# LayerNorm and MLP on one core: tile 2 turned by VectorE, eight rows opened with tiles 0 and 1, tile 3 of twenty rows made up later

## The chip, the core and the metric

The kernel runs on one core of a Trainium2 chip. The metric is the device time of one execution in microseconds (us). In the names of the profile PE is TensorE, PEld its weight loads, DVE is VectorE, ACT is ScalarE, POOL is GpSimd and SP is SyncE, which issues most of the DMAs. All times of a trace count from the start of its span.

## The reference

```
def reference(x, w1, b1, w2, b2):      # x 2048 x 1024, w1 1024 x 3584, w2 3584 x 1024, bfloat16
    y = _layernorm(x, axis=-1)         # (x - mean) / sqrt(var + 1e-5)
    h = _gelu(jnp.einsum("bsd,df->bsf", y, w1) + b1)     # tanh approximation
    return jnp.einsum("bsf,fd->bsd", h, w2) + b2
```

## The kernel before

**Blocks, tiles, rows.** The 2048 positions of x are cut into 4 blocks of 512, a block into 4 tiles of 128. For each block the first product (helper `pe_cell`, L331) makes h transposed: 28 *rows* r of 128 features, each a PSUM bank of 128 x 512, the sum over 8 slices *dt* of the 1024 inputs. A matmul holds a 128 x 128 piece of w1 still and streams columns of the transposed input `yT_sb`; a column is a position, so a tile is 128 columns. ScalarE applies gelu and bias b1 (`act_gelu`, L351) and writes `hT_sb`. The second product (`out_chunk`, L380) sums over 28 rows into 128 x 512 pieces of the output, which VectorE adds b2 to (L391) and SP stores. The order on TensorE is: first product of block 0, second product of block 0, first of block 1, and so on.

**Queues.** The program is written as one list of operations for each engine, in order. An operation waits for named events of others; what stands behind it on its engine waits too. SP's list holds the loads: the halves of tiles 0 and 1 first, then 256 KB pieces of w1 (`w1_chunks`) with tiles 2 and 3 of x in between, b1, the rest of w1, block 1 of x, w2, b2 and the other blocks.

**The opening.** Block 0 is special, because its input has to be normalised and transposed while w1 still arrives. Tiles 0 to 3 are only centred before the product (`raw_tile`: a sum on VectorE at L413, a subtraction at L417, into `c_sb`); the division by the standard deviation comes after it. ScalarE's `square` (L423) or VectorE's statistics give the variance, GpSimd takes the power -0.5 (L236, L426, L429), and VectorE spreads the four tiles' results over all partitions into `rbc_sb` with transposes and copies (L462, L467, L472). When a row's bank is complete, VectorE multiplies it in place by `rbc_sb` (L348, event `rm_r`), and the gelu of the row waits for that. Ahead of rbc on VectorE stand the turn of b1 (L457) and its cast.

Tiles 0, 1 and 2 are transposed by TensorE (`pe_T`, L305; each group of slices is copied from PSUM by ScalarE, L311). Tile 3 is turned on VectorE by one instruction that transposes each 32 x 32 block (L439), and 16 copies of 32 partitions put the blocks in place, 8 on VectorE (L448), 8 on ScalarE (L453).

TensorE runs 39 matmuls on constants first (`fill`, L291). `OPEN` then lists the order: an entry (t, d0, d1) is tile t with slices d0 to d1 for the four rows of the first wave, an entry (t, None) the transposes of tile t. Rows 4 to 7 follow with tiles 0 to 2 together (384 columns), then tile 3 of rows 0 to 7, which completes them. Rows 8 to 27 take all 512 columns at once. A row takes a bank from `new_unit`: rows 0 to 7 the banks 0 to 7, later ones the six banks 0 to 5 in turn, waiting for the gelu that last read the bank.

**VectorE's planner.** From rm 0 on VectorE's order is planned on the host. `crit` holds the multiplications (later the b2 additions) with a due time, `fills` the normalisation and the turn of the next block with a release time; the planner takes the next of `crit` when its due time has come within 0.3 us of its own clock, otherwise the next of `fills`. Due times come from the estimate `est` of when TensorE completes the row.

Of the kernel before, what the change touches and what calls it, by code (L numbers as in the profile page):

```python
# [11 lines left out]
P = 128  # L12
# [4 lines left out]
R0 = 4  # L17
R1 = 8
N_FILL_A = 37
N_FILL_C = 2  # L20
OPEN = ((0, 0, 2), (1, None), (0, 2, 4), (0, 4, 6), (1, 0, 6), (0, 6, 8), (2, None), (1, 6, 8), (2, 0, 8))
CEN_0 = (0, 2, 8)
GROUPS_0 = ((0, 2, 7), (2, 5, 4), (5, 8, 5))
GROUPS_1 = ((0, 4, 6), (4, 8, 7))
GROUPS_2 = ((0, 2, 4), (2, 5, 5), (5, 8, 6))
COPY_ACT = ((0, 1), (0, 2), (0, 3), (1, 2), (1, 3), (2, 3), (3, 2), (2, 1))
NOB = 2
# [59 lines left out]
def bass_standalone__mixer_channel_mlp__prompt_kernel(  # L87
# [18 lines left out]
    HC = D // 2  # L106
    NRAW = TPB
    assert ST % TB == 0 and NB >= 2 and D % P == 0 and D & (D - 1) == 0 and F % P == 0 and D % NCH == 0
    assert HC <= 512 and DT == 8 and FT >= 8 and FT <= 32

    w1_chunks = [(j, j + 2, 0, 512) for j in range(0, DT, 2)] + [(j, j + 4, 512, 768) for j in (0, 4)]
    c0 = 768
    for wdt in (256, 512, 1024, 1024):
        if c0 + wdt <= F:
            w1_chunks.append((0, DT, c0, c0 + wdt))
            c0 += wdt
# [20 lines left out]
    with ExitStack() as es:  # L137
# [62 lines left out]
        for i in range(2):  # L200
            for h, q in enumerate((sp, act)):
                dma(x_sb[:, i, h * HC:(h + 1) * HC], xf[i * P:(i + 1) * P, h * HC:(h + 1) * HC],
                    f"x{i}_{h}", P * HC * 2, q)
        for ci in range(3):
            load_w1(ci)
        load_x_tile(2)
        load_w1(3)
        load_x_tile(3)
        load_w1(4)
        load_w1(5)  # L210
        sp.op(None, waits=["b1z"])
        dma(b1r_sb[0:FT, :], b1.rearrange("(t p) -> t p", p=P), "b1", F * 2)
        for ci in range(6, len(w1_chunks)):
            load_w1(ci)
# [109 lines left out]

        def pe_cell(b, r, t0, t1, bank, waits, sig, dts=None):
            n0, n1 = t0 * P, t1 * P
            dts = list(range(DT)) if dts is None else list(dts)
            for k, dt in enumerate(dts):
                w = (list(waits) if k == 0 else []) + [f"w1c{w1_chunk_of(r, dt)}"]
                w += [v for t in range(t0, t1) for v in yT_ev[b * TPB + t][dt].split("+")]  # L330
                pe.op(lambda e, b=b, r=r, dt=dt, n0=n0, n1=n1, bank=bank: e.matmul(  # L331
                    ps[:, bank, n0:n1], lhsT=w1_sb[:, dt, r * P:(r + 1) * P], rhs=yT_sb[:, b % 2, dt, n0:n1],
                    start=(dt == 0 and t0 == 0), stop=(dt == DT - 1 and t1 == TPB)),
                    waits=w, sig=(sig if dt == DT - 1 else None))
            pe_t[0] += len(dts) * _mm_us(n1 - n0)
            if dts[-1] == DT - 1 and sig is not None:
                est[sig] = pe_t[0]

        hT_row = {}
        crit = []  # L340

        def act_gelu(b, r, bank, sig):
            ev = sig
            if b == 0:
                ev = f"rm_{r}"
                n = NRAW * P
                rb = rbc_sb[:, :, :].rearrange("p i t -> p (i t)")
                crit.append((est[sig], (lambda e, bank=bank: e.tensor_tensor(  # L348
                    out=ps[:, bank, 0:n], in0=ps[:, bank, 0:n], in1=rb, op=ALU.mult),
                    [sig, "rbc"], ev, 0.66), 0))  # L350
            act.op(lambda e, r=r, bank=bank: e.activation(  # L351
                out=hT_sb[:, r, :], in_=ps[:, bank, :], func=ACT.Gelu_apprx_tanh,
                bias=b1_sb[:, r:r + 1], scale=1.0),
# [12 lines left out]
        grp_oe = []  # L366
        fills = []
        store_last = {}

        def out_chunk(b, st, c0, c1, region, prev_store):  # L370
# [17 lines left out]
            if prev_store is not None:  # L388
# [11 lines left out]
        act.op(lambda e: e.preload_act_table(ACT.Gelu_apprx_tanh))  # L400
        act.op(lambda e: e.activation(out=o_sb[:, 0, 0:HC], in_=x_sb[:, 0, 0:HC], func=ACT.Copy, scale=1.0 / D,
                                      accum_out=sum_sb[:, 0:1]), waits=["x0_0"], sig="sa0")
        dve_put((lambda e: e.tensor_scalar(out=o_sb[:, 0, HC:D], in0=x_sb[:, 0, HC:D], scalar1=1.0 / D, scalar2=0.0,  # L403
                                           op0=ALU.mult, op1=ALU.add, accum_out=sum_sb[:, 1:2]),
# [7 lines left out]
        def raw_tile(i, xw):  # L412
            dve_put((lambda e: e.scalar_tensor_tensor(out=o_sb[:, 0, HC:D], in0=x_sb[:, i, 0:HC], scalar=1.0,  # L413
                                                      in1=x_sb[:, i, HC:D], op0=ALU.mult, op1=ALU.add,
# [93 lines left out]

# [91 lines left out]
```

## Time and profile before

| | |
|---|---|
| median of 3 runs | 397.84 us (397.46 to 397.89) |
| the profiled execution | 397.33 us, span 396.1 us |
| granted TensorE clock | 1.00 |
| TensorE busy | 393.0 us, 2011 matmuls |
| VectorE, ScalarE, GpSimd busy | 160.1, 88.3, 10.4 us |
| first matmul of the first product | 5.90 us |
| first rm | 18.08 us |
| last piece of block 1 of x waited for by VectorE until | 30.86 us |

A span is the time from the first to the last instruction of the program; the time of the execution has 1.2 us more around it. A row of the timeline gives start, length, engine, line, operation, output <- inputs, shapes and how many instructions were merged into it, and in brackets how long the engine stood idle ahead of it and what ended that. A row of stretches gives the stretch, its length, the busy time with the count of instructions that touch it, the granted clock and the DMA's share and rate.

### The profile page before, as it was taken

How to read it: one execution, taken by the hardware profiler on the slowest of the kernel's cores; microseconds unless marked ns; L12 is line 12 of the kernel's file. 1: busy time of each engine (PE TensorE's matmuls, PEld its weight loads, DVE VectorE, ACT ScalarE, POOL GpSimd, SP SyncE). 2: the span in 40 equal slices, each digit the busy share in tenths (PEclk: the TensorE clock that was granted, in tenths of full speed). 3: DMA queues.
4: the chain of work that ended last, by engine and by line, in shares of the span. 5: the costliest groups of instructions: out<-in, count | busy, mean ns of one | idle time of the engine just before them, and what ended most of it. 6: DMA issues, size and time to landing. Idle time of an engine off the chain costs nothing.

```text
span 396.1 us, 4673 instructions
## 1 busy us (share of the span) xinstructions
PE 393.0 (99%) x2011; PEld 187.8 (47%) x2011; DVE 160.1 (40%) x341; ACT 88.3 (22%) x137; POOL 10.4 (3%) x28
## 2 busy tenths in 40 slices
PE   8999999999999999999999999999999999999998
PEld 8754444444444444444444444444444444444445
DVE  5958898988999405987100000001100000001011
ACT  6663330000143342000023443100003334400000
POOL 1201100001000100000000000000000000000000
PEclk9999999999999999999999999999999999999999
DMA  8999940000000000000000000000000000000000
GB/s 264 355 386 388 384 163 15 26 26 16 26 0 2 0 2 0 27 17 24 26 15 0 0 2 0 13 15 26 22 19 13 2 0 0 2 13 26 15 26 28
DMA packets 17358, 23.64 MB, mean 60 GB/s; under 512 B 1082, under 2 KB 9786, under 8 KB 17338
## 3 DMA queue, kind: packets, MB, share of 16 engines
q1 hardware_dynamic: 17050, 23.08, 16.7%
q8 instruction: 16, 0.26, 0.3%
q10 hardware_dynamic: 288, 0.26, 0.2%
q14 instruction: 4, 0.03, 0.0%
HBM read 19.14 MB, written 4.19 MB: 59 GB/s over the span
## 4 chain that ended last, share of the span: by engine, by line
PE 98%; DMA 1%; SPq 0%; DVE 0%; issue 0%
PE ps L331 49%; PE ps L380 49%; DMA w_sb<-in_w_dram 1%; PE ps L305 0%; SPq L178 0%; DVE o_sb L391 0%
## 5 line engine op out<-in xcount | busy, mean ns | idle before, releaser
L331 PE MATMUL ps<-yT_sb,w_sb 128*128 128x512 bf16 (+2 forms) x1024 | 194.8, 353 | 0.3 <-DMA w_sb<-in_w_dram 0.3
L380 PE MATMUL ps<-w_sb,hT_sb 128*128 128x512 bf16 (+2 forms) x924 | 194.1, 373 | 0.0
L331 PEld LDWEIGHTS ps<-yT_sb,w_sb 128*128 128x128 bf16 x1024 | 93.4, 98 | 100.7 <-DMA w_sb<-in_w_dram 0.5
L380 PEld LDWEIGHTS ps<-w_sb,hT_sb 128*128 128x128 bf16 x924 | 89.2, 98 | 104.6
L351 ACT ACTIVATE hT_sb<-ps,b_sb 128x512 bf16<-128x512 f32 x112 | 76.3, 687 | 254.6 <-PE ps L331 231.6
L391 DVE TENSOR_TENSOR o_sb<-ps,b_sb 128x512 bf16<-128x512 f32 (+2 forms) x33 | 22.3, 676 | 198.8 <-PE ps L380 198.7
L278 DVE STREAM_TRANSPOSE yT_sb<-x_sb 32x256 bf16<-32x256 bf16 x192 | 83.7, 436 | 20.7 <-PE ps L331 17.7
L348 DVE TENSOR_TENSOR ps<-ps,rbc_sb 128x512 f32<-128x512 f32 x28 | 18.8, 697 | 6.1 <-PE ps L331 5.3
L231 DVE BATCH_NORM_STATS2 st_sb<-x_sb 128x6 f32<-128x512 bf16 x26 | 17.2, 671 | 0.4 <-DMA x_sb<-in_x_dram 0.3
L236 POOL TENSOR_TENSOR rstd_sb<-mv_sb,nhalf 128x1 f32<-128x1 f32 x12 | 6.6, 548 | 114.4 <-DVE mv_sb L239 114.4
L246 DVE TENSOR_SCALAR x_sb<-x_sb,mv_sb,rstd_sb 128x1024 bf16<-128x1024 bf16 x12 | 6.5, 544 | 2.5 <-POOL rstd_sb L236 2.0
L291 PE MATMUL ps<-const-bfloat16-1.0 128*128 128x128 bf16 x39 | 4.3, 305 | 0.8 <-PEq L585 0.8
L291 PEld LDWEIGHTS ps<-const-bfloat16-1.0 128*128 128x128 bf16 x39 | 4.0, 142 | 0.8 <-issue 0.8
L311 ACT COPY yT_sb<-ps 128x384 bf16<-128x384 bf16 (+2 forms) x8 | 3.4, 484 | 1.5 <-PE ps L305 1.5
L423 ACT ACTIVATE hT_sb<-x_sb,sum_sb 128x1024 bf16<-128x1024 bf16 x3 | 3.5, 1162 | 0.0
L453 ACT COPY yT_sb<-o_sb 32x256 bf16<-32x256 bf16 x8 | 3.2, 401 | 0.1
L239 DVE BATCH_NORM_AGGREGATE mv_sb<-st_sb 128x2 f32<-128x15 f32 x13 | 2.9, 219 | 0.8
L413 DVE SCALAR_TENSOR_TENSOR o_sb<-x_sb 128x512 bf16<-128x512 bf16 x3 | 2.1, 698 | 0.7 <-DMA x_sb<-in_x_dram 0.6
L403 DVE TENSOR_SCALAR_CACHE_REDUCE o_sb<-x_sb 128x512 bf16<-128x512 bf16 x1 | 0.7, 686 | 3.5 <-DMA x_sb<-in_x_dram 3.5
L305 PE MATMUL ps<-ident,c_sb 128*128 128x128 bf16 x24 | 2.0, 220 | 0.0
L429 POOL TENSOR_TENSOR rs_sb<-ve_sb,nhalf 128x1 f32<-128x1 f32 x3 | 1.9, 645 | 0.3
L448 DVE COPY yT_sb<-o_sb 32x256 bf16<-32x256 bf16 x8 | 1.8, 222 | 0.1
(26 smaller groups left out, 13.9 us busy)
## 6 DMA issues: line engine op xcount, KB each, us to landing
w_sb<-in_w_dram SPq DMA_DIRECT2D x4, 1792.0 KB, 18.4
w_sb<-in_w_dram SPq DMA_DIRECT2D x2, 2048.0 KB, 15.1
out_dram<-o_sb SPq DMA_DIRECT2D x31, 128.0 KB, 1.7
x_sb<-in_x_dram SPq DMA_DIRECT2D x3, 1024.0 KB, 14.4
w_sb<-in_w_dram SPq DMA_DIRECT2D x6, 256.0 KB, 4.7
w_sb<-in_w_dram SPq DMA_DIRECT2D x1, 1024.0 KB, 10.2
x_sb<-in_x_dram SPq DMA_DIRECT2D x2, 256.0 KB, 4.9
w_sb<-in_w_dram SPq DMA_DIRECT2D x1, 512.0 KB, 6.5
```

The lines of the kernel that those rows point to most:

```text
L231: return (lambda e, i=i, h=h: e.bn_stats(st_sb[:, i, 6 * h:6 * (h + 1)], x_sb[:, i, h * HC:(h + 1) * HC]), [x_ev.get(i, f"x{i}_{h}")], f"s ...
L236: pool.op(lambda e, i=i, to=to: e.tensor_tensor(out=to[:, i:i + 1], in0=mv_sb[:, i, 1:2], in1=nhalf[:, i:i + 1], op=ALU.pow), waits=[f"mv{ ...
L246: return (lambda e, i=i: e.tensor_scalar(out=x_sb[:, i, :], in0=x_sb[:, i, :], scalar1=mv_sb[:, i, 0:1], scalar2=rstd_sb[:, i:i + 1], op0= ...
L278: res.append((lambda e, src=src, dst=dst: e.transpose(out=dst, in_=src), waits, (f"tr{i}" if lastop else None), 0.47))
L291: pe.op(lambda e: e.matmul(ps[:, 0, 0:P], lhsT=one, rhs=one, start=True, stop=True), waits=[gate] if gate else [])
L311: act.op(lambda e, dst=dst, psrc=psrc: e.copy(out=dst, in_=psrc), waits=[f"tp{i}_{j0}"], sig=f"te{i}_{j0}")
L331: pe.op(lambda e, b=b, r=r, dt=dt, n0=n0, n1=n1, bank=bank: e.matmul(ps[:, bank, n0:n1], lhsT=w1_sb[:, dt, r * P:(r + 1) * P], rhs=yT_sb[: ...
L348: crit.append((est[sig], (lambda e, bank=bank: e.tensor_tensor(out=ps[:, bank, 0:n], in0=ps[:, bank, 0:n], in1=rb, op=ALU.mult), [sig, "rb ...
L351: act.op(lambda e, r=r, bank=bank: e.activation(out=hT_sb[:, r, :], in_=ps[:, bank, :], func=ACT.Gelu_apprx_tanh, bias=b1_sb[:, r:r + 1], ...
L380: pe.op(lambda e, st=st, ft=ft, c0=c0, c1=c1, bank=bank: e.matmul(ps[:, bank, 0:c1 - c0], lhsT=hT_sb[:, ft, st * P:(st + 1) * P], rhs=w2_s ...
L391: crit.append((est[sig], (lambda e, ob=ob, c0=c0, c1=c1, bank=bank: e.tensor_tensor(out=o_sb[:, ob, c0:c1], in0=ps[:, bank, 0:c1 - c0], in ...
L423: act.op(lambda e, i=i: e.activation(out=hT_sb[:, 2 * i:2 * i + D // TB, :].rearrange("p a b -> p (a b)"), in_=x_sb[:, i, :], func=ACT.Squ ...
```

## The change

Tile 2 is no longer transposed by TensorE. A new helper `turn_ops` makes the block transpose on VectorE and the 16 copies, nine on VectorE and seven on ScalarE. Tile 3 leaves the opening: it is normalised in full with statistics like the later blocks' tiles and turned by `turn_ops` with all 16 copies on VectorE, as `fills` of the planner. `rbc_sb` covers three tiles (NRAW is 3).

`OPEN` now takes slices 0 to 2 of tile 0 for four rows, tile 1's transposes, slices 2 to 5 of tile 0, slices 0 to 5 of tile 1, and slices 5 to 8 of both together. Rows 4 to 7 follow with tiles 0 and 1 in one (256 columns), then tile 2 of rows 0 to 7, then rows 8 to 19 with tiles 0 to 2 (384 columns). Tile 3 of rows 0 to 19 comes after that, in groups of four rows to a bank, in banks 6 and 7 by turns; each row's quarter has a gelu of 128 columns of its own. Rows 20 to 27 take 512 columns as before. The rm's of rows 0 to 7 get due times from `T_DVE_START` and `AHEAD`, those of rows 8 to 19 are due `RM_LATE` after the estimate.

The loads are ordered by `LOADS`: w1's pieces 0 and 1, tile 2, pieces 2 to 7 (all 256 KB, columns 0 to 1023), tile 3, then b1 and the rest. Scratch outputs of the sums move from `o_sb` to `hT_sb`, since `o_sb` holds the two turned tiles; `pe_cell` can end a bank's sum before the fourth tile.

```diff
@@ -18,18 +18,21 @@
 R1 = 8
 N_FILL_A = 37
 N_FILL_C = 2
-OPEN = ((0, 0, 2), (1, None), (0, 2, 4), (0, 4, 6), (1, 0, 6), (0, 6, 8), (2, None), (1, 6, 8), (2, 0, 8))
+OPEN = ((0, 1, 0, 2), (1, None), (0, 1, 2, 5), (1, 2, 0, 5), (0, 2, 5, 8))
 CEN_0 = (0, 2, 8)
 GROUPS_0 = ((0, 2, 7), (2, 5, 4), (5, 8, 5))
 GROUPS_1 = ((0, 4, 6), (4, 8, 7))
-GROUPS_2 = ((0, 2, 4), (2, 5, 5), (5, 8, 6))
-COPY_ACT = ((0, 1), (0, 2), (0, 3), (1, 2), (1, 3), (2, 3), (3, 2), (2, 1))
+COPY_ACT = ((0, 1), (0, 2), (0, 3), (1, 2), (1, 3), (2, 3), (3, 2))
+LOADS = (0, 1, -2, 2, 3, 4, 5, 6, 7, -3)
+ROWS_3 = 20
+AHEAD = 2
+RM_LATE = 4.0
 NOB = 2
 TAIL_CUTS = (0, 384, 512)
 N_W2_CHUNKS = 4
 
 T_PE_START = 5.7
-T_DVE_START = 19.5
+T_DVE_START = 15.7
 DMA_T0 = 2.6
 DMA_BYTES_PER_US = 0.34e6
@@ -104,13 +107,13 @@
     NCH = min(512, D)
     DH = D // NCH
     HC = D // 2
-    NRAW = TPB
+    NRAW = TPB - 1
     assert ST % TB == 0 and NB >= 2 and D % P == 0 and D & (D - 1) == 0 and F % P == 0 and D % NCH == 0
     assert HC <= 512 and DT == 8 and FT >= 8 and FT <= 32
 
-    w1_chunks = [(j, j + 2, 0, 512) for j in range(0, DT, 2)] + [(j, j + 4, 512, 768) for j in (0, 4)]
-    c0 = 768
-    for wdt in (256, 512, 1024, 1024):
+    w1_chunks = [(j, j + 2, c, c + 512) for c in (0, 512) for j in range(0, DT, 2)]
+    c0 = 1024
+    for wdt in (512, 1024, 1024):
         if c0 + wdt <= F:
             w1_chunks.append((0, DT, c0, c0 + wdt))
             c0 += wdt
@@ -201,16 +204,11 @@
             for h, q in enumerate((sp, act)):
                 dma(x_sb[:, i, h * HC:(h + 1) * HC], xf[i * P:(i + 1) * P, h * HC:(h + 1) * HC],
                     f"x{i}_{h}", P * HC * 2, q)
-        for ci in range(3):
-            load_w1(ci)
-        load_x_tile(2)
-        load_w1(3)
-        load_x_tile(3)
-        load_w1(4)
-        load_w1(5)
+        for o in LOADS:
+            load_x_tile(-o) if o < 0 else load_w1(o)
         sp.op(None, waits=["b1z"])
         dma(b1r_sb[0:FT, :], b1.rearrange("(t p) -> t p", p=P), "b1", F * 2)
-        for ci in range(6, len(w1_chunks)):
+        for ci in range(8, len(w1_chunks)):
             load_w1(ci)
         load_x_block(1)
         for ci in range(nw2c):
...
@@ -338,18 +336,21 @@
 
         hT_row = {}
         crit = []
-
-        def act_gelu(b, r, bank, sig):
+        fills = []
+
+        def act_gelu(b, r, bank, sig, nt=TPB):
             ev = sig
             if b == 0:
                 ev = f"rm_{r}"
                 n = NRAW * P
                 rb = rbc_sb[:, :, :].rearrange("p i t -> p (i t)")
-                crit.append((est[sig], (lambda e, bank=bank: e.tensor_tensor(
+                due = T_DVE_START + max(0, r - AHEAD) * NRAW * DT * _mm_us(P) if r < R1 else est[sig] + (
+                    RM_LATE if r < ROWS_3 else 0.0)
+                crit.append((max(est[sig], due), (lambda e, bank=bank: e.tensor_tensor(
                     out=ps[:, bank, 0:n], in0=ps[:, bank, 0:n], in1=rb, op=ALU.mult),
-                    [sig, "rbc"], ev, 0.66), 0))
-            act.op(lambda e, r=r, bank=bank: e.activation(
-                out=hT_sb[:, r, :], in_=ps[:, bank, :], func=ACT.Gelu_apprx_tanh,
+                    [sig, "rbc"], ev, 0.47), 0))
+            act.op(lambda e, r=r, bank=bank, nt=nt: e.activation(
+                out=hT_sb[:, r, 0:nt * P], in_=ps[:, bank, 0:nt * P], func=ACT.Gelu_apprx_tanh,
                 bias=b1_sb[:, r:r + 1], scale=1.0),
                 waits=[ev, "b1c"], sig=f"g_{b}_{r}")
             bank_gelu[bank] = f"g_{b}_{r}"
...
@@ -433,25 +433,30 @@
         raw_tile(1, ["x1_0", "x1_1"])
         dve_put(op_stats(0, 0))
         dve_put(op_stats(0, 1))
+        def turn_ops(i, src, y, copy_act):
+            k = i - 2
+            res = [(lambda e: e.transpose(out=o_sb[:, k, :], in_=src), [y], f"t{i}", 1.3)]
+            tv = o_sb[:, k, :].rearrange("p (j q s) -> p j q s", j=DT, q=4)
+            acts = []
+            for tq in range(4):
+                for q in range(4):
+                    a = tv[32 * tq:32 * (tq + 1), :, q, :]
+                    d = yT_sb[32 * q:32 * (q + 1), 0, :, i * P + 32 * tq:i * P + 32 * (tq + 1)]
+                    if (tq, q) in copy_act:
+                        acts.append((a, d))
+                    else:
+                        res.append((lambda e, a=a, d=d: e.tensor_copy(out=d, in_=a), [f"t{i}"],
+                                    f"tc{i}" if (tq, q) == (3, 3) else None, 0.25))
+            assert (3, 3) not in copy_act
+            yT_ev[i] = [f"tc{i}" + (f"+ta{i}" if acts else "")] * DT
+            return res, acts
+
         raw_tile(2, ["x2"])
+        t2_dve, t2_act = turn_ops(2, c_sb[:, 2, :], "y2", COPY_ACT)
+        dve_put(t2_dve[0])
         dve_put(op_aggr(0, rs_sb))
-        raw_tile(3, ["x3"])
-        dve_put((lambda e: e.transpose(out=o_sb[:, 0, :], in_=c_sb[:, 3, :]), ["y3"], "t3"))
-        tv = o_sb[:, 0, :].rearrange("p (j q s) -> p j q s", j=DT, q=4)
-        c3_act, c3_dve = [], []
-        for tq in range(4):
-            for q in range(4):
-                src = tv[32 * tq:32 * (tq + 1), :, q, :]
-                dst = yT_sb[32 * q:32 * (q + 1), 0, :, 3 * P + 32 * tq:3 * P + 32 * (tq + 1)]
-                (c3_act if (tq, q) in COPY_ACT else c3_dve).append((src, dst))
-        for k, (src, dst) in enumerate(c3_dve):
-            dve_put((lambda e, src=src, dst=dst: e.tensor_copy(out=dst, in_=src), ["t3"],
-                     "tc3" if k == len(c3_dve) - 1 else None))
-
-        def t3_act():
-            for k, (src, dst) in enumerate(c3_act):
-                act.op(lambda e, src=src, dst=dst: e.copy(out=dst, in_=src), waits=["t3"],
-                       sig="ta3" if k == len(c3_act) - 1 else None)
+        for o in t2_dve[1:]:
+            dve_put(o)
 
         for q in range(4):
             dve_put((lambda e, q=q: e.transpose(out=b1h_sb[32 * q:32 * (q + 1), :],
@@ -482,35 +487,60 @@
         pe_t[0] = T_PE_START
         wave = [new_unit() for _ in range(R0)]
         for st in OPEN:
-            t = st[0]
             if st[1] is None:
-                for g in (GROUPS_2 if t == 2 else GROUPS_1):
-                    pe_T(t, g, c_sb[:, t, :])
-                if t == 1:
-                    square(1)
-                    square(2)
-                else:
-                    square(3)
-                    t3_act()
+                for g in GROUPS_1:
+                    pe_T(1, g, c_sb[:, 1, :])
+                square(1)
+                square(2)
+                for k, (a, d) in enumerate(t2_act):
+                    act.op(lambda e, a=a, d=d: e.copy(out=d, in_=a), waits=["t2"],
+                           sig="ta2" if k == len(t2_act) - 1 else None)
                 continue
-            for dt in range(st[1], st[2]):
+            t0, t1, d0, d1 = st
+            for dt in range(d0, d1):
                 for r in range(R0):
-                    pe_cell(0, r, t, t + 1, wave[r][0], wave[r][1] if t == 0 and dt == 0 else [], None, dts=[dt])
+                    pe_cell(0, r, t0, t1, wave[r][0], wave[r][1] if t0 == 0 and dt == 0 else [], None, dts=[dt])
         wave += [new_unit() for _ in range(R0, R1)]
-        for r0 in range(R0, R1, 2):
+        for dt in range(DT):
+            for r in range(R0, R1):
+                pe_cell(0, r, 0, 2, wave[r][0], wave[r][1] if dt == 0 else [], None, dts=[dt])
+        for r in range(R1):
+            pe_cell(0, r, 2, 3, wave[r][0], [], f"m1_0_{r}", end=True)
+            act_gelu(0, r, wave[r][0], f"m1_0_{r}", NRAW)
+        for r in range(R1, ROWS_3):
+            bank, uw = new_unit()
+            pe_cell(0, r, 0, 3, bank, uw, f"m1_0_{r}", end=True)
+            act_gelu(0, r, bank, f"m1_0_{r}", NRAW)
+        rel3 = est["x3"]
+        y_ev[3] = ["y3"] * DT
+        t3_dve, _ = turn_ops(3, x_sb[:, 3, :], "y3", ())
+        for o in [op_stats(3, 0), op_stats(3, 1), op_aggr(3), op_norm(3)] + t3_dve:
+            fills.append((rel3, o, 1))
+        for r in range(ROWS_3):
+            k = r % TPB
+            bank = NRING + (r // TPB) % 2
+            waits = [bank_gelu[bank]] if k == 0 else []
+            last = k == TPB - 1 or r == ROWS_3 - 1
             for dt in range(DT):
-                for r in (r0, r0 + 1):
-                    pe_cell(0, r, 0, 3, wave[r][0], wave[r][1] if dt == 0 else [], None, dts=[dt])
-        yT_ev[3] = ["tc3+ta3"] * DT
-        for r in range(R1):
-            pe_cell(0, r, 3, 4, wave[r][0], [], f"m1_0_{r}")
-            act_gelu(0, r, wave[r][0], f"m1_0_{r}")
+                w = (waits if dt == 0 else []) + [f"w1c{w1_chunk_of(r, dt)}"] + yT_ev[3][dt].split("+")
+                pe.op(lambda e, r=r, dt=dt, k=k, bank=bank, last=last: e.matmul(
+                    ps[:, bank, k * P:(k + 1) * P], lhsT=w1_sb[:, dt, r * P:(r + 1) * P],
+                    rhs=yT_sb[:, 0, dt, 3 * P:TB], start=(k == 0 and dt == 0), stop=(dt == DT - 1 and last)),
+                    waits=w, sig=(f"m1t_{r}" if dt == DT - 1 else None))
+                pe_t[0] += _mm_us(P)
+            if last:
+                for rr in range(r - k, r + 1):
+                    act.op(lambda e, rr=rr, c=(rr - r + k) * P, bank=bank: e.activation(
+                        out=hT_sb[:, rr, 3 * P:TB], in_=ps[:, bank, c:c + P], func=ACT.Gelu_apprx_tanh,
+                        bias=b1_sb[:, rr:rr + 1], scale=1.0), waits=[f"m1t_{r}"], sig=f"gt_{rr}")
+                    hT_row[(0, rr)] = f"gt_{rr}"
+                bank_gelu[bank] = f"gt_{r}"
 
         def mm1_rows(b, r0):
             for r in range(r0, FT):
                 mm1_row(b, r)
 
-        mm1_rows(0, R1)
+        mm1_rows(0, ROWS_3)
         for b in range(NB):
             if b + 1 < NB:
                 tiles = list(range((b + 1) * TPB, (b + 2) * TPB))
```

More of the change, by code (lines that the diff above doesn't have):

```diff
@@ L323, in new_unit, with pe_cell @@
             return bank, ([w] if w else [])
-        def pe_cell(b, r, t0, t1, bank, waits, sig, dts=None):
+        def pe_cell(b, r, t0, t1, bank, waits, sig, dts=None, end=False):
             n0, n1 = t0 * P, t1 * P
@@ L332, in pe_cell @@
                     ps[:, bank, n0:n1], lhsT=w1_sb[:, dt, r * P:(r + 1) * P], rhs=yT_sb[:, b % 2, dt, n0:n1],
-                    start=(dt == 0 and t0 == 0), stop=(dt == DT - 1 and t1 == TPB)),
+                    start=(dt == 0 and t0 == 0), stop=(dt == DT - 1 and (end or t1 == TPB))),
                     waits=w, sig=(sig if dt == DT - 1 else None))
@@ L366, in bass_standalone__mixer_channel_mlp__prompt_kernel @@
         grp_oe = []
-        fills = []
         store_last = {}
@@ L400, in bass_standalone__mixer_channel_mlp__prompt_kernel @@
         act.op(lambda e: e.preload_act_table(ACT.Gelu_apprx_tanh))
-        act.op(lambda e: e.activation(out=o_sb[:, 0, 0:HC], in_=x_sb[:, 0, 0:HC], func=ACT.Copy, scale=1.0 / D,
+        act.op(lambda e: e.activation(out=hT_sb[:, 2 * NRAW, :], in_=x_sb[:, 0, 0:HC], func=ACT.Copy, scale=1.0 / D,
                                       accum_out=sum_sb[:, 0:1]), waits=["x0_0"], sig="sa0")
-        dve_put((lambda e: e.tensor_scalar(out=o_sb[:, 0, HC:D], in0=x_sb[:, 0, HC:D], scalar1=1.0 / D, scalar2=0.0,
+        dve_put((lambda e: e.tensor_scalar(out=hT_sb[:, 2 * NRAW + 1, :], in0=x_sb[:, 0, HC:D], scalar1=1.0 / D, scalar2=0.0,
                                            op0=ALU.mult, op1=ALU.add, accum_out=sum_sb[:, 1:2]),
@@ L412, in raw_tile @@
         def raw_tile(i, xw):
-            dve_put((lambda e: e.scalar_tensor_tensor(out=o_sb[:, 0, HC:D], in0=x_sb[:, i, 0:HC], scalar=1.0,
+            dve_put((lambda e: e.scalar_tensor_tensor(out=hT_sb[:, 2 * NRAW + 1, :], in0=x_sb[:, i, 0:HC], scalar=1.0,
                                                       in1=x_sb[:, i, HC:D], op0=ALU.mult, op1=ALU.add,
```

## The prediction

> **What bounds the kernel now.** I read the page first, for the busiest engine and the chain that ended last.
>
> ```profile
> PE 393.0 (99%) x2011; PEld 187.8 (47%) x2011; DVE 160.1 (40%) x341; ACT 88.3 (22%) x137; POOL 10.4 (3%) x28
> PE 98%; DMA 1%; SPq 0%; DVE 0%; issue 0%
> ```
>
> TensorE is both. Next came the same chain in order of time (start, length, what).
>
> ```profile
> 1.69 4.16 DMA w_sb<-in_w_dram
> 5.85 0.05 issue
> 5.90 0.62 PE ps L331 x8
> ...
> 10.09 45.61 PE ps L331 x296
> 55.70 48.35 PE ps L380 x224
> ```
>
> TensorE waits until 5.85 for the first piece of w1, starts at 5.90 and never again rests for long. Nothing after block 0's first product (its second product starts at 55.5) is changed, so the whole effect is the shift of that start. A piece of w1 that nobody moves fixes the beginning. I therefore need the price of a matmul by width, from the busy time of stretches, and the opening of VectorE (DVE) and ScalarE (ACT) from the timeline.
>
> ```profile
> 12.23:17.42 5.19, 5.19 (x35) 1.00 1.07 364
> 17.43:20.99 3.56, 3.56 (x65) 1.00 1.05 387
> ```
>
> The stretches hold 32 matmuls of 384 columns and 64 of 128 (the counts include neighbours that reach in): 0.162 and 0.0556 each. 224 of 512 take 48.35, 0.216 each. That is a fixed 0.0023 and 0.417 ns a column; one of 256 is then 0.109.
>
> ```profile
> 6.05 1.28 DVE L231 BATCH_NORM_STATS2 st_sb<-x_sb 128x6 f32<-128x512 bf16 x2
> 7.92 0.69 DVE L413 SCALAR_TENSOR_TENSOR o_sb<-x_sb 128x512 bf16<-128x512 bf16 x1 [0.58 <-DMA x_sb<-in_x_dram]
> ...
> 13.84 0.90 DVE L457 STREAM_TRANSPOSE b1h_sb<-b1r_sb 32x32 bf16<-32x32 bf16 x4
> ...
> 18.08 5.55 DVE L348 TENSOR_TENSOR ps<-ps,rbc_sb 128x512 f32<-128x512 f32 x9
> ...
> 47.10 0.70 DVE L348 TENSOR_TENSOR ps<-ps,rbc_sb 128x512 f32<-128x512 f32 x1
> 47.83 0.89 DVE L278 STREAM_TRANSPOSE yT_sb<-x_sb 32x256 bf16<-32x256 bf16 x2
> ```
>
> Three things to see: tile 2 (fourth 256 KB piece on the queue) lands at 7.9; the row multiplications (L348, "rm" below) begin only when rbc is there, 4.24 after the b1 turn began; and an rm takes 0.60 start to start among wide instructions but 0.73 ahead of a 32-partition one.
>
> **TensorE's own work.** Eight PE transposes of tile 2 go: -8 x 0.0556 = -0.44. Block 0 has 352 matmuls before and 468 after (264 of 128 columns, 44 of 256, 96 of 384, 64 of 512), with the same columns in all: 116 x 0.0023 = +0.27. From 5.90 to 55.54 is 49.64, of which the matmuls and 16 transposes are 49.5, so small pauses of about 0.1 may go too. Even if every new wait were nil the gain is about 0.3, under 0.1%; 0.2% (0.8 us) is about what a measurement of this kernel can tell from no change.
>
> **A wait for w1's third piece.** LOADS puts tile 2 ahead of piece 2, so piece 2 takes the fourth place and lands at about 7.9 instead of before 7.25. TensorE has until then 8 matmuls, 8 transposes of tile 1 and 8 matmuls: 5.90 + 24 x 0.0556 = 7.23. The next, dt 4 of tile 0, needs piece 2 and starts at 7.95: +0.72. The 20 matmuls of tile 1 that could run meanwhile stand behind it in the in-order queue. Bounds: 0 if the third and fourth pieces should land together, 0.9 if the queue is slower; I take 0.72, from the landing seen.
>
> **Eight rows with tiles 0 and 1.** From 7.95: 24 x 0.0556 + 12 x 0.109 + 32 x 0.109 = 6.13, so tile 2 is wanted at 14.1. The pieces for rows 4 to 7 hide behind this: the six 256 KB pieces of before landed 0.70 apart (5.85 to 9.37), so the eighth of w1 is there at 11.5, wanted at 13.2. Tile 2 itself: DVE is free at 7.27, needs 1.28 to the turn (as tile 3 did, 9.37 to 10.65), 1.28 for it, 0.25 for a statistic and 9 copies at 0.234: done at 12.2. ACT has two squares until 10.1 and 7 copies at 0.41: 13.0. Hidden by 1.1; without this cover TensorE would pay what exceeds 14.1. Rows 0 to 7 with tile 2 take 64 x 0.0556 and end at 17.64.
>
> **The first rm.** b1 is now issued behind ten pieces, not eight: 5.85 + 9 x 0.70 = 12.15, and b1 shortly after; no row shows its landing, bounds 12.2 and 12.9, I take 12.45. DVE stands there in order, with all rm's behind it. The 4.24 from there shrinks by a quarter of the width of the ten rbc instructions, to 3.9 (bounds 3.8 and 4.1): rm 0 at 16.35. An rm on 384 columns saves 0.133 (the additions at the end of the kernel: 0.69 for 512 columns, 0.29 for 128), so 0.57 and 0.47 start to start. Its gelu follows 0.60 after its start (0.73 between 18.08 and 18.81 before) and lasts 0.58: row 0's bank is free at 17.6, row 8 wants it at 17.64. No wait, but no slack either (bounds 0 and 0.5).
>
> **Where the forecast decides: row 19's rm.** After row 8's start, 12 rows x 8 x 0.162 end at 33.2, tile 3 of rows 0 to 7 at 36.8. Rows 8 to 11 then reuse bank 6, which waits for the gelus of rows 0 to 3's fourth quarter. These stand on ACT behind the gelu of row 19, and that behind rm 19. DVE's queue order follows from the planner's due times (RM_LATE is 4 us for rows 8 to 19, while tile 3's normalisation, turn and 16 copies fill in, and block 1's from 30.4 on): between rm 0 and rm 19 I count 12 rm's ahead of wide instructions at 0.465, 7 ahead of narrow ones at 0.60, 5 halves of statistics at 0.61, the first aggregate with the stop for GpSimd's power 0.93 (9.06 to 9.92 before, and its handover), another 0.13, two normalisations at 0.46, the turn 1.28 and 16 copies at 0.236: 19.9. All of their inputs are there by then, so the sum is the queue itself. rm 19 starts at 36.25, its gelu at 36.85.
>
> ACT then runs one gelu of 384 and four of 128. Copies on ACT took 588 ns for 512 columns and 368 for 256, so 0.86 ns a column; two of 512 in a row overlap by 0.1. From the gelu's 687 ns at 512, 384 columns take 0.58 and 128 take 0.36, spaced 0.48 and 0.26: 0.48 + 3 x 0.26 + 0.36 = 1.62. TensorE goes on at 38.5 instead of 36.8: +1.7. Bounds: 0 (no loss of overlap ahead of the copies, 7 x 0.13; gelus spaced as the copies' slope; rm 0 at 16.1) and 3.0 (rm 0 at 16.8, gelus end to end, the rm's after statistics at 0.67). I take 1.7, since every step has a row near it. The Trainium skill, "ScalarE: Activation LUTs", What ACT_TABLE_LOAD costs, gives an activation with a bias pointer about 280 ns plus 0.833 ns an element and an overlap of about 93 ns. By that the five would need 1.78 and the sum below would be 0.15 more; the trace has 687 for the page's 706 at 512 columns and no gelu of 128.
>
> Tile 3's own turn is hidden: its 16th copy ends 4.3 before rm 19, at 32, wanted at 33.2. Row 14 wants the bank of row 8 at 25.4; rm 8, 7.8 after rm 0, gives it free at about 25.4. What also goes, tile 2's three PSUM copies on ACT (10.01 to 11.13) and tile 3's square with its two GpSimd steps, kept nobody waiting on TensorE: 0. The last 12 small rows and rows 20 to 27 wait for nothing: four small gelus (1.1) fit into four small rows (1.79). Pieces 8 to 10 carry the same bytes ahead of them as before, when the 1 MB landed by 17.0; wanted at 17.6.
>
> **The sum.** -0.44 + 0.27 - 0.1 + 0.72 + 1.7 = +2.2 (rounded). The profiled execution took 397.33 (span 396.1; the 1.2 around it is not touched), so 399.5 by its own time; the median of the runs, 397.84, lies 0.5 above it, and since a median is forecast I add to that: 400.0.
>
> **Rivals.** (1) No bank wait: rm 19 is 1.7 earlier, because DVE overlaps its narrow copies or ACT its small gelus better. Only the third piece stays: +0.45, 398.3, within the bound, so not slower; decided from the point where row 19's gelu begins before 35.1. For it: 0.60 once ahead of a narrow instruction (45.60 to 46.20); against: 0.73 the other times. 0.22. (2) Nothing waits, not even for the third piece: 397.5. Against: the 7.92 row. 0.04, half of it counted as faster, to be careful. (3) DVE late from b1 on: rm 0 0.5 later and the queue 0.8 longer make rows 8 and 14 wait too, and bank 6 until 39.8: 401.3. For it: the two slacks near nothing. 0.17. (4) A pause costs clock. The kernel's first filler matmuls come 0.11 apart (33 in 3.68) though the granted clock reads 1.00, half speed; the 0.5 us pause ahead of 5.90 cost none. If the bank wait brought that state back for as long as it held at the start, 3.7, half of that would be lost: 401.8. 0.03. The Trainium skill, "TensorE: Matmul & The Clock Gate", Part 1, has the clock halved after an idle window of about 3.4 us; by that a pause of 1.7 is too short. The trace shows no pause that long.
>
> **Chances.** Forecast 0.54. Slower by over 0.2%: 0.54 + 0.17 + 0.03 = 0.74. Within 0.2%: 0.22 + 0.02 = 0.24. Faster: 0.02. The range goes from just under rival 1 to just over rival 3, 398.0 to 401.5.
>
> **What would show it.** In the changed profile: TensorE idle about 0.7 before a matmul at 7.95, released by a w1 transfer; rm 0 at 16.3; no pause near 14.1; a pause of over 1 us near 37 on L331's successor for tile 3, released by ACT; ACT's gelu of row 19 starting near 36.9; second product's start 2.2 later than 55.5. Wrong if the 37 pause is missing, or if a pause stands where I have none, at tile 2 or at row 20.

## The result and the profile after

The changed kernel took 399.58 us (median of 5 runs, 398.64 to 400.12) against 397.84 (5 runs, 397.31 to 398.41): ratio 1.0039, 95% interval 1.0024 to 1.0054, so 1.0 to 2.1 us slower. The profiled execution took 399.76, span 398.5. TensorE's rows of the timeline (start, length, engine, line; in brackets its idle time ahead and what ended it); L329 is the first product, L526 tile 3 of rows 0 to 19, L380 the second product:

```profile
6.57 0.62 PE L329 MATMUL ps<-yT_sb,w_sb 128*128 128x128 bf16 x8 [0.79 <-DMA w_sb<-in_w_dram]
...
8.74 25.60 PE L329 MATMUL ps<-yT_sb,w_sb 128*128 128x128 bf16 x228 [0.67 <-DMA w_sb<-in_w_dram]
34.18 3.74 PE L526 MATMUL ps<-yT_sb,w_sb 128*128 128x128 bf16 x64
38.83 5.53 PE L526 MATMUL ps<-yT_sb,w_sb 128*128 128x128 bf16 x96 [0.92 <-ACT hT_sb L533]
44.20 13.98 PE L329 MATMUL ps<-yT_sb,w_sb 128*128 128x512 bf16 x64
58.02 2.32 PE L380 MATMUL ps<-w_sb,hT_sb 128*128 128x512 bf16 x10
```

Two waits are new: for w1's third piece ahead of 8.74, and for the gelus of tile 3's first group (L533) ahead of 38.83, after 64 matmuls, where bank 6 is used again. From start to start, where an idle row does not count the matmul's own length, they are 0.83 and 1.08. A third, of 0.10, stands ahead of row 8 inside the long row. The second product started at 55.54 in the kernel before:

```profile
55.54 2.75 PE L380 MATMUL ps<-w_sb,hT_sb 128*128 128x512 bf16 x12
```

It starts 58.02 - 55.54 = 2.48 later. Of this 0.67 is the first matmul itself, at 6.57 instead of 5.90, and 1.81 lies between the first matmul and the second product (51.45 against 49.64).

VectorE (DVE) and ScalarE (ACT) around the two ends of the path, from the same timeline:

```profile
13.33 0.90 DVE L462 STREAM_TRANSPOSE b1h_sb<-b1r_sb 32x32 bf16<-32x32 bf16 x4 [0.76 <-DMA b1r_sb<-in_b_dram]
...
17.33 1.96 DVE L349 TENSOR_TENSOR ps<-ps,rbc_sb 128x384 f32<-128x384 f32 x4
...
36.58 0.56 DVE L349 TENSOR_TENSOR ps<-ps,rbc_sb 128x384 f32<-128x384 f32 x1
37.17 0.58 ACT L352 ACTIVATE hT_sb<-ps,b_sb 128x384 bf16<-128x384 f32 x1 [0.34 <-DVE ps L349]
37.65 2.16 ACT L533 ACTIVATE hT_sb<-ps,b_sb 128x128 bf16<-128x128 f32 x8
```

VectorE stood 0.76 for b1, began the row multiplications (rm) at 17.33 and came to row 19's at 36.58; its gelu and four small ones follow, and TensorE goes on at 38.83.

### The profile page after: what moved, and what is told of

Its sections match the earlier page's. It is cut to its first block, busy times and chain, and to the rows that moved or that the text cites. A ratio compares the mean times of both kernels' runs of the same rounds, so it can differ in the third digit from the quotient of the medians.

```text
span 398.5 us, 4922 instructions
## 1 busy us (share of the span) xinstructions
PE 393.3 (99%) x2119; PEld 194.6 (49%) x2119; DVE 161.2 (40%) x360; ACT 89.1 (22%) x151; POOL 10.0 (3%) x27
## 4 chain that ended last, share of the span: by engine, by line
PE 92%; DVE 5%; DMA 1%; SPq 1%; issue 1%; ACT 0%; POOL 0%
PE ps L380 49%; PE ps L329 42%; DVE ps L349 2%; PE ps L526 1%; DMA w_sb<-in_w_dram 1%; DVE yT_sb L448 1%; DVE st_sb L229 1%; SPq L181 1%; DVE o_sb L438 0%; ACT hT_sb L533 0%; DVE x_sb L244 0%; ACT hT_sb L352 0%; POOL rstd_sb L234 0%; DVE mv_sb L237 0%; DVE o_sb L391 0%
## 5 line engine op out<-in xcount | busy, mean ns | idle before, releaser
L380 PE MATMUL ps<-w_sb,hT_sb 128*128 128x512 bf16 (+2 forms) x924 | 194.1, 373 | 0.0
L329 PE MATMUL ps<-yT_sb,w_sb 128*128 128x512 bf16 (+3 forms) x980 | 186.3, 352 | 1.5 <-DMA w_sb<-in_w_dram 1.5
L380 PEld LDWEIGHTS ps<-w_sb,hT_sb 128*128 128x128 bf16 x924 | 89.3, 98 | 104.4
L329 PEld LDWEIGHTS ps<-yT_sb,w_sb 128*128 128x128 bf16 x980 | 91.5, 98 | 95.1 <-DMA w_sb<-in_w_dram 1.8
L352 ACT ACTIVATE hT_sb<-ps,b_sb 128x512 bf16<-128x512 f32 (+1 forms) x112 | 74.3, 668 | 253.2 <-PE ps L329 231.6
L229 DVE BATCH_NORM_STATS2 st_sb<-x_sb 128x6 f32<-128x512 bf16 x28 | 18.5, 670 | 0.1
L349 DVE TENSOR_TENSOR ps<-ps,rbc_sb 128x384 f32<-128x384 f32 x28 | 15.1, 557 | 3.1 <-PE ps L329 2.8
L526 PE MATMUL ps<-yT_sb,w_sb 128*128 128x128 bf16 x160 | 9.3, 219 | 0.9 <-ACT hT_sb L533 0.9
L526 PEld LDWEIGHTS ps<-yT_sb,w_sb 128*128 128x128 bf16 x160 | 9.0, 98 | 1.2 <-ACT hT_sb L533 1.1
L533 ACT ACTIVATE hT_sb<-ps,b_sb 128x128 bf16<-128x128 f32 x20 | 5.6, 377 | 2.3 <-PE ps L526 2.3
L448 DVE COPY yT_sb<-o_sb 32x256 bf16<-32x256 bf16 x25 | 5.4, 218 | 0.4
L309 ACT COPY yT_sb<-ps 128x384 bf16<-128x384 bf16 (+2 forms) x5 | 2.3, 503 | 2.0 <-PE ps L303 2.0
L423 ACT ACTIVATE hT_sb<-x_sb,sum_sb 128x1024 bf16<-128x1024 bf16 x2 | 2.3, 1152 | 0.0
```

Of the source, the lines that this page charges most:

```text
L229: return (lambda e, i=i, h=h: e.bn_stats(st_sb[:, i, 6 * h:6 * (h + 1)], x_sb[:, i, h * HC:(h + 1) * HC]), [x_ev.get(i, f"x{i}_{h}")], f"s ...
L349: crit.append((max(est[sig], due), (lambda e, bank=bank: e.tensor_tensor(out=ps[:, bank, 0:n], in0=ps[:, bank, 0:n], in1=rb, op=ALU.mult), ...
L352: act.op(lambda e, r=r, bank=bank, nt=nt: e.activation(out=hT_sb[:, r, 0:nt * P], in_=ps[:, bank, 0:nt * P], func=ACT.Gelu_apprx_tanh, bia ...
L380: pe.op(lambda e, st=st, ft=ft, c0=c0, c1=c1, bank=bank: e.matmul(ps[:, bank, 0:c1 - c0], lhsT=hT_sb[:, ft, st * P:(st + 1) * P], rhs=w2_s ...
L448: res.append((lambda e, a=a, d=d: e.tensor_copy(out=d, in_=a), [f"t{i}"], f"tc{i}" if (tq, q) == (3, 3) else None, 0.25))
L526: pe.op(lambda e, r=r, dt=dt, k=k, bank=bank, last=last: e.matmul(ps[:, bank, k * P:(k + 1) * P], lhsT=w1_sb[:, dt, r * P:(r + 1) * P], rh ...
```

## The experiments

The theory (A): block 0's end is set by VectorE's queue, from b1's landing through rm 0 to rm 19, and not by the sum of TensorE's waits. Rival B: each wait of TensorE simply adds its length. Two smaller rivals: C, that the late first matmul belongs to the change; D, that bank 6 waits because of the small gelus themselves. Since the first matmul moves from execution to execution, I compare profiles by three stretches: F, from the first matmul of the first product to the second product; R, from rm 0 to the second product; and TensorE's waits, start to start. A dash stands for a wait under 0.1.

| profile | first matmul | third piece | row 8 | bank 6 | F | R |
|---|---|---|---|---|---|---|
| before | 5.90 | - | - | - | 49.64 | |
| after | 6.57 | 0.83 | 0.10 | 1.08 | 51.45 | 40.69 |
| e1 (after again) | 5.70 | 0.79 | 0.11 | 1.08 | 51.48 | 40.68 |
| e2 (rows 16 to 19 due at once) | 5.97 | 0.68 | 0.18 | - | 50.36 | 39.60 |
| e3 (third piece first) | 6.42 | - | 0.75 | 1.08 | 51.34 | 40.69 |
| e4 (b1 early) | 6.64 | 1.11 | - | 0.50 | 51.04 | 40.70 |
| e5 (RM_LATE 6) | 6.04 | 0.91 | 0.16 | 2.40 | 54.94 | 43.59 |
| e7 (all three treated) | 6.23 | - | 0.27 | - | 50.15 | 39.59 |
| e8 (before, tile 2 earlier) | 5.93 | 0.96 | - | - | 50.75 | |
| e9 (tile 2 by TensorE) | 6.64 | 0.85 | - | - | 50.72 | 41.27 |
| e10 (before again) | 6.01 | - | - | - | 49.70 | |
| e11 (after, third time) | 6.26 | 0.69 | 0.28 | 1.07 | 51.48 | 40.67 |

**e1, the changed kernel again.** No edit.

> The changed kernel once more, nothing edited. Theory A (VectorE's queue from b1's landing to row 19's multiplication sets block 0's end; TensorE's earlier waits are absorbed in it): the third piece of w1 is again waited for, 0.7 to 0.9, and bank 6 at tile 3's ninth row again, 1.0 to 1.7; the first matmul of the first product may start anywhere from 5.9 to 6.6, with the landing of w1's first piece, since no load ahead of that piece was moved. Rival B (each of TensorE's waits adds its own length): the same waits. Rival C (the late start of 6.57 in the changed kernel's profile comes from the change): 6.5 or later again. Time 399.0 to 400.0 by all.

Measured: 398.89 (12 runs, 398.60 to 400.02), ratio 1.0020, interval 1.0004 to 1.0035. The first matmul starts at 5.70, so the late start of 6.57 does not come with the change each time, and C falls in that form; both the start and the time lie just under what all theories had expected. The waits are the same to 0.04.

**e2, the last four rows' multiplications due at once.**

```diff
-                    RM_LATE if r < ROWS_3 else 0.0)
+                    RM_LATE if r < ROWS_3 - TPB else 0.0)
```

> The multiplications of rows 16 to 19 are due when TensorE has made the row, not 4 us later; VectorE's order changes for them alone (block 1's statistics go behind row 19's). Theory A: row 19's multiplication starts at about 34.3 instead of 36.6, the gelus of tile 3's first group run when their matmuls are done, the wait for bank 6 (1.08 in the changed kernel's profile) is gone and no other takes its place; second product's start and the time 1.0 to 1.2 earlier, about 398.5. Rival B: the same. Rival D (the wait at bank 6 belongs to the small gelus themselves, their length or the group of four): the wait stays over 0.7 and the time within 0.3 of the changed kernel.

Measured: 398.33 (12 runs), ratio 0.9997, interval 0.9979 to 1.0014. ScalarE's timeline in this kernel:

```profile
32.26 2.70 ACT L352 ACTIVATE hT_sb<-ps,b_sb 128x384 bf16<-128x384 f32 x5 [0.74 <-DVE ps L349]
35.57 1.14 ACT L533 ACTIVATE hT_sb<-ps,b_sb 128x128 bf16<-128x128 f32 x4 [0.60 <-PE ps L526]
37.35 1.14 ACT L533 ACTIVATE hT_sb<-ps,b_sb 128x128 bf16<-128x128 f32 x4 [0.64 <-PE ps L526]
```

and TensorE's:

```profile
33.58 9.10 PE L526 MATMUL ps<-yT_sb,w_sb 128*128 128x128 bf16 x160
```

All 160 small matmuls run in one piece, and the small gelus now wait for TensorE. R falls by 1.08, the whole wait: bank 6 waited for the place of row 19's multiplication in VectorE's queue, and D falls. The median is 0.56 under e1's on the same chip, less than the 1.1 in the profiles; the runs of each scatter by 1.4 to 1.9.

**e3, w1's third piece ahead of tile 2.**

```diff
-LOADS = (0, 1, -2, 2, 3, 4, 5, 6, 7, -3)
+LOADS = (0, 1, 2, -2, 3, 4, 5, 6, 7, -3)
```

> Tile 2 is loaded behind w1's third piece instead of ahead of it. Theory A: TensorE's wait of 0.83 for the piece falls under 0.15, but VectorE starts tile 2 about 0.7 later, the first multiplication stays where b1 and rbc put it or comes up to 0.3 later, row 8 now waits 0.7 to 1.1 for row 0's gelu, bank 6 waits as long as before, and the time is within 0.3 of the changed kernel: 399.3 to 399.9. Rival B: 0.8 earlier, 398.8.

Measured: 399.39 (12 runs), ratio 1.0033, interval 1.0017 to 1.0049. TensorE's timeline:

```profile
7.33 10.39 PE L329 MATMUL ps<-yT_sb,w_sb 128*128 128x128 bf16 x140
18.31 15.77 PE L329 MATMUL ps<-yT_sb,w_sb 128*128 128x384 bf16 x96 [0.58 <-ACT hT_sb L352]
```

The wait for the piece is gone, and row 8 now waits 0.75 for row 0's gelu; F changes by 0.1, R not at all. This is where A and B part: B wanted 0.8, and the median is 0.50 over e1's on the same chip, not under it. VectorE no longer stands for b1 (its turn starts at 13.07 with no idle time) but comes later from tile 2, so rm 0 has the same distance to the first matmul as in the changed kernel within 0.15.

**e4, b1 early.**

```diff
-LOADS = (0, 1, -2, 2, 3, 4, 5, 6, 7, -3)
+LOADS = (0, 1, -2, 2, 3, "b1", 4, 5, 6, 7, -3)
...
```

The rest of the edit issues b1's DMA at its place in the loop.

> b1 (7 KB) is loaded behind w1's fourth piece instead of behind ten pieces of 256 KB; nothing else moves. Theory A: VectorE's wait of 0.76 for b1 is gone, the first multiplication starts at 16.4 to 16.7 instead of 17.33, row 8's wait of 0.1 is gone, row 19's multiplication starts 0.6 to 0.8 earlier and the wait for bank 6 falls from 1.08 to 0.4 to 0.6; time 0.6 to 0.8 earlier, 398.9. Rival B: TensorE never waited for b1, so at most 0.1 earlier, 399.5.

Measured: 398.68 (12 runs), ratio 1.0010, interval 0.9995 to 1.0025. rm 0 comes 10.34 after the first matmul instead of 10.76, R stays at 40.70, and F falls by 0.41, all of it by rm 0, although TensorE waits for nothing of b1. That speaks for A against B. It is only half of the gain expected: VectorE no longer waits for b1 but for tile 2, which it takes up 1.71 after the first matmul (8.35 - 6.64) instead of 1.40 (7.97 - 6.57), and from there to rm 0 it does not wait again. w1's third piece was late too, by 1.11 in this execution, so TensorE came later to bank 6 as well, where the wait fell to 0.50.

```profile
8.35 0.69 DVE L415 SCALAR_TENSOR_TENSOR hT_sb<-x_sb 128x512 bf16<-128x512 bf16 x1 [0.82 <-DMA x_sb<-in_x_dram]
...
12.98 0.90 DVE L464 STREAM_TRANSPOSE b1h_sb<-b1r_sb 32x32 bf16<-32x32 bf16 x4
...
38.49 5.53 PE L528 MATMUL ps<-yT_sb,w_sb 128*128 128x128 bf16 x96 [0.34 <-ACT hT_sb L535]
```

**e5, RM_LATE 6 instead of 4.**

```diff
-RM_LATE = 4.0
+RM_LATE = 6.0
```

> RM_LATE is 6 us instead of 4, so VectorE puts more of tile 3's and block 1's work ahead of the late multiplications. Theory A: from the first multiplication to row 19's it is 20.6 instead of 19.25; row 14 waits 0.2 to 0.5 for row 8's gelu, bank 6 waits 1.9 to 2.4 instead of 1.08, and the second product starts 41.8 to 42.3 after the first multiplication (40.7 in the changed kernel): 1.2 to 1.6 slower, about 400.4. Rival D (the small gelus themselves): bank 6 as before, 1.1.

Measured: 401.25 (4 runs, 400.13 to 402.73), ratio 1.0080, interval 1.0055 to 1.0105. From rm 0 to rm 19 it is 38.02 - 17.39 = 20.63, as counted, and bank 6 waits 2.40; row 14's wait came out at 0.04. But R is 43.59, not 42. (F holds one more wait, of 0.42 for w1's second piece, ahead of rm 0.) The rows of stretches (length, TensorE's busy time and matmuls, granted clock, DMA) show why:

```profile
36.00:38.00 2.00, 2.00 (x37) 1.00 1.06 388
38.00:40.00 2.00, 0.02 (x1) 1.00 1.06 387
40.26:42.00 1.74, 1.74 (x17) 0.50 1.04 379
42.00:43.00 1.00, 1.00 (x12) 0.50 1.06 387
43.00:44.00 1.00, 1.00 (x17) 0.74 1.05 385
44.00:46.00 2.00, 2.00 (x40) 1.00 1.06 389
```

```profile
40.26 7.07 PE L526 MATMUL ps<-yT_sb,w_sb 128*128 128x128 bf16 x96 [2.24 <-ACT hT_sb L533]
```

After the pause the granted clock is 0.50 until 43.5, and the same 96 matmuls take 7.07 instead of 5.53: 1.54 more. Without them R would be 42.05, inside the expectation. The profiled execution is the slowest of the four: in it and in the one of 401.69 the mean granted clock is 0.996, in the other two, 400.13 and 400.81, it is 1.00, and they lie nearer to the 400.4 expected.

**e7, all three waits treated.** e2's edit, w1's third piece ahead of tile 2, b1 right behind w1's first piece, and on VectorE b1's turn and cast moved, unchanged, ahead of tile 2:

```diff
+LOADS = (0, "b1", 1, 2, -2, 3, 4, 5, 6, 7, -3)
...
+        for q in range(4):
+            dve_put((lambda e, q=q: e.transpose(out=b1h_sb[32 * q:32 * (q + 1), :],
...
         raw_tile(2, ["x2"])
```

> The changed kernel with its three waits treated at once: w1's third piece ahead of tile 2, b1 right behind w1's first piece and turned on VectorE ahead of tile 2, multiplications of rows 16 to 19 due at once. Theory A: no wait at the third piece, row 8 waits 0 to 0.4, none at bank 6; from the first matmul of the first product to the second product 49.4 to 49.9 (before 49.64, changed kernel 51.45), so equal to the kernel before within 0.3 and 1.6 to 2.0 under the changed kernel at the same start. If more than 0.5 is still lost, something other than these three waits costs time.

Measured: 398.13 (12 runs, 397.92 to 398.82), ratio 1.0001, interval 0.9991 to 1.0012: equal to the kernel before, and not better than it. F is 50.15, 0.25 over the expectation and 0.51 over the kernel before, just over the 0.5 above which something other than the three waits was to blame. Of the three, 0.27 at row 8 and 0.07 at the third piece are left, and a new one of 0.38 came at tile 2: it landed at 8.29, VectorE, still at b1's turn and cast, took it up at 8.63, and ScalarE's seven copies, which TensorE then waits for, follow that. These 0.72, less the 0.20 that TensorE's own work saves, make the 0.51. On VectorE's timeline, rbc now waits for GpSimd's last power:

```profile
8.63 0.68 DVE L415 SCALAR_TENSOR_TENSOR hT_sb<-x_sb 128x512 bf16<-128x512 bf16 x1
...
13.84 0.27 DVE L469 STREAM_TRANSPOSE rbc_sb<-rs_sb 32x96 f32<-32x96 f32 x1 [0.61 <-POOL rs_sb L431]
```

**e8, the kernel before with tile 2 loaded ahead of w1's third piece.**

```diff
-        for ci in range(3):
+        for ci in range(2):
             load_w1(ci)
         load_x_tile(2)
+        load_w1(2)
         load_w1(3)
```

> The kernel before, with tile 2 loaded ahead of w1's third piece and nothing else changed. Here VectorE's queue does not set row 8 (its first multiplications were done 1.5 before row 8 started). Theory A: TensorE waits 0.7 to 0.85 for the third piece and keeps all of it: from the first matmul to the second product 50.3 to 50.5 instead of 49.64, time 0.7 slower, 398.5. If a later wait or slack could take it back, less than 0.3.

Measured: 398.36 (10 runs), ratio 1.0012, interval 0.9999 to 1.0025, so not clear by time. In the profile the wait is kept: 0.96, and F is 1.11 over the kernel before (four of the first matmuls also came at half rate, 0.2 together). In the profile, where VectorE's queue does not set row 8, the same swap costs its whole price.

```profile
8.45 2.41 PE L332 MATMUL ps<-yT_sb,w_sb 128*128 128x128 bf16 x40 [0.80 <-DMA w_sb<-in_w_dram]
```

**e9, tile 2 by TensorE again, b1 early.**

```diff
+OPEN = ((0, 1, 0, 2), (1, None), (0, 1, 2, 5), (1, 2, 0, 5), (2, None), (0, 2, 5, 8))
...
+GROUPS_2 = ((0, 2, 4), (2, 5, 5), (5, 8, 6))
...
+LOADS = (0, 1, -2, 2, 3, "b1", 4, 5, 6, 7, -3)
...
-        dve_put(t2_dve[0])
         dve_put(op_aggr(0, rs_sb))
-        for o in t2_dve[1:]:
-            dve_put(o)
...
```

> The changed kernel with tile 2 turned by TensorE again (8 transposes behind tile 1's slices, copies from PSUM on ScalarE), no block transpose and no 9 + 7 copies for it, and b1 loaded behind w1's fourth piece; all else, RM_LATE too, as changed. Theory A: VectorE comes to the first multiplication about 1 earlier against the first matmul, row 8's wait is gone, bank 6 waits under 0.3, and the third piece is still waited for (0.7 to 0.9): from the first matmul to the second product 50.5 to 50.9 against 51.45, so 0.6 to 0.9 faster than the changed kernel in spite of 0.45 more on TensorE. Rival B: the 0.45 of transposes is simply added, 51.9.

Measured: 398.87 (10 runs), ratio 1.0022, interval 1.0010 to 1.0034. F is 50.72: 0.73 less than the changed kernel with 0.45 more work on TensorE. VectorE's queue is now ahead; rm 0 waits 1.22 for TensorE, and TensorE waits for the third piece alone. Two edits are in this run; e4, with b1 alone, has F at 51.04, so what taking tile 2 off VectorE gives beside it is 0.32 in these two profiles.

```profile
16.09 1.96 DVE L352 TENSOR_TENSOR ps<-ps,rbc_sb 128x384 f32<-128x384 f32 x4 [1.22 <-PE ps L332]
```

**e10 and e11, both kernels again.** No edit.

> The kernel before once more. The question is what one profile's start is worth: the first matmul of the first product follows the landing of w1's first piece, at 5.90 in the first profile of this kernel and at 5.70 to 6.64 in those of the changed one. If the landing varies from execution to execution alike in both kernels, the start lies anywhere from 5.7 to 6.7 and from it to the second product it is 49.5 to 49.7 whatever the start. If the change itself delays the landing, it is 5.9 within 0.1 again.

> The changed kernel for the third time, on the chip of the run before. Start anywhere from 5.7 to 6.7; from the first multiplication of VectorE to the second product 40.7 within 0.03, as in the three profiles so far that keep its order; bank 6 waits 1.08 where row 8 waits for row 0's gelu. Time 0.7 to 1.9 over the kernel before, depending on the starts.

Measured: 397.88 (12 runs, ratio to the other runs of the same kernel 0.9995, interval 0.9981 to 1.0009) and 399.41 (12 runs, ratio 1.0027, interval 1.0012 to 1.0042). F is 49.70 and 51.48, R 40.67. The start of 6.01 in e10 fits both readings of its expectation. The chain that ended last, in order of time, names in e11 the path of the changed kernel: from b1's transfer over rbc, the multiplications and the gelus to bank 6.

```profile
7.04 6.00 DMA b1r_sb<-in_b_dram
14.11 0.27 DVE rbc_sb L467
...
17.07 1.96 DVE ps L349 x4
...
36.89 0.58 ACT hT_sb L352
37.48 1.04 ACT hT_sb L533 x4
38.56 5.53 PE ps L526 x96
```

In the first profile of the changed kernel the same view goes back from rm 0 to TensorE's matmuls and w1's third piece instead. But row 0's last matmul starts at 15.29 there, long before rm 0 at 17.33, and rm 0 follows VectorE's previous instruction by 0.10, as in every profile of this kernel and its variants but e9: VectorE's own queue holds it.

The first matmul lay at 5.90, 6.01 and 5.93 in the three profiles of before and its variant, and at 5.70 to 6.64 in the nine of the changed kernel and its variants. It follows the landing of w1's first piece by 0.05 in eight of the twelve; in e1, e2, e5 and e10 the piece landed earlier, and the first matmul starts behind tile 0's transposes. Whether the change moves its mean is left open: both profiled executions of before (397.33 and 397.46) were faster than that kernel's medians in the comparisons (397.84 to 398.19), so their starts need not be typical.

## Why the prediction was right, point by point

**The verdict and its mechanism held.** Slower by 2.2 was forecast; the medians differ by 1.74, F by 1.81. TensorE's own work with its pauses, the third piece, row 8 and the bank wait were put at -0.27, 0.72, 0 and 1.7 and came out as -0.20, 0.83, 0.10 and 1.08: the last fell short by 0.6, and the other three made up 0.28 of that, which is luck. In time the size is less sure than the sign: in the later comparisons the medians of the same two kernels differ by 0.70 (e1) and 1.27 (e11). R is 40.67 to 40.70 in five profiles (after, e1, e3, e4, e11) in which the first matmul moved by 0.9 and two other waits came and went, and it moved only where VectorE's order or, in e9, its load was changed. (In e5, 1.54 of the move is the clock's.) That is the step of row 19's rm.

**TensorE's own work** was right. In e2, with its two waits and one small pause of 0.06 taken off, F is 50.36 - 0.68 - 0.18 - 0.06 = 49.44, against 49.58 for before without its pause of 0.06: -0.14, with -0.17 forecast. The pauses thought to go were 0.06, not 0.1.

**The third piece** was sized well, 0.72 for 0.83 (0.68 to 1.11 in the others). As an account of the time the sum is right, since the bank wait in it was counted from TensorE's arrival with the third piece's wait already in. But the term cannot be taken away by itself, which the text does not say: e3 took the wait away and gained 0.1, and the time came back at row 8. Where the bank wait is gone, as in rival 1 and in e2, the third piece does stay: F of e2 is 0.72 over the kernel before. Two gates stood within 0.1 of each other at row 8, as the step of the first rm said, and the text should have drawn from it that opening one alone gives next to nothing.

**The first rm** was put 10.45 after the first matmul; it is 10.76 to 10.81. b1's turn starts 6.76 after the first matmul (13.33 - 6.57) where 6.55 was taken (12.45 - 5.90), and from its turn to rm 0 it was 4.00, not 3.9. So row 8 waits 0.10 to 0.28 where none was forecast.

**The bank wait** is the mis-sized term: 1.08 for 1.7. From row 19's gelu on the count was right: 38.83 - 37.17 = 1.66 against 1.65 (38.5 - 36.85), and four small gelus take 1.14 as spaced. From rm 0 to rm 19 the queue took 36.58 - 17.33 = 19.25 instead of 19.9:

```profile
22.79 0.56 DVE L349 TENSOR_TENSOR ps<-ps,rbc_sb 128x384 f32<-128x384 f32 x1
23.25 1.24 DVE L438 STREAM_TRANSPOSE o_sb<-x_sb 128x1024 bf16<-128x1024 bf16 x1
24.41 1.46 DVE L349 TENSOR_TENSOR ps<-ps,rbc_sb 128x384 f32<-128x384 f32 x3
25.78 0.20 DVE L448 COPY yT_sb<-o_sb 32x256 bf16<-32x256 bf16 x1
25.91 0.55 DVE L349 TENSOR_TENSOR ps<-ps,rbc_sb 128x384 f32<-128x384 f32 x1
```

Ahead of the turn the spacing is 0.46, the turn takes 1.16, not 1.28, and a lone copy 0.13, not 0.24: instructions overlapped here that did not in the rows the prices came from. Over the whole stretch the 16 copies took 3.54 for 3.78, the turn 0.12 less, the multiplications 9.66 for 9.78 and the rest 0.14 less. TensorE reached the bank 20.42 after rm 0 (37.75 - 17.33), as forecast (36.8 - 16.35).

**Rival 4** did not happen in the changed kernel, whose longest pause was 0.92 idle. e5 shows that it is nearer than the text had it, and its price: 1.54 in the profiled execution, where half of 3.7 was counted.

## What to carry to other kernels

Waits on the busiest engine cannot be taken away one by one while another engine's in-order queue feeds it at several places: find that queue and measure from its first fixed point (here rm 0) to the end; a stretch that stays constant while other waits come and go is the path. Moving work from the full engine to a less busy one can cost when it goes to the front of a queue that releases the full engine's buffers, and a due time that is late for one buffer can hold another that is queued behind it. Where two gates open within 0.1 us of each other, as at row 8, opening one of them gives next to nothing, since the other keeps the start: against the first matmul, row 8 began 0.1 earlier in e3 and no earlier in e4 (where the third piece was also later; e4's gain of 0.41 came at bank 6).

## What the runs showed of the hardware that was not expected

With a TensorE pause of 2.24 us the granted clock was halved: in the profiled execution of e5 it was 0.50 from the first matmul after the pause to 43.5, and 30 matmuls of 128 columns came 0.106 apart instead of 0.056. The Trainium skill, "TensorE: Matmul & The Clock Gate", Part 1, has the clock fall after an idle window of about 3.4 us; here less was enough, and TensorE had been busy until 38.0. Pauses of 0.92 in the changed kernel cost nothing. That the pause alone decides is not shown: two of e5's four executions read 1.00 and were not profiled, and one of e9's ten reads 0.996, though its profiled one has no wait at bank 6. Whether there is a bound between 0.92 and 2.24 was not tried.

The first piece of w1 landed at 4.99 to 6.59 in the twelve profiles, with the same loads issued ahead of it in all. TensorE's first matmul moved by 0.9 (5.70 to 6.64), which is half of the whole effect. How much of the scatter of the runs this makes was not measured.
